# Retention and two MLPs on one core: the first two token blocks by halves of F, and all GpSimd arithmetic moved to VectorE

## The chip, the cores and the metric

The kernel runs on one core of a Trainium2 chip. A core has a matrix engine (TensorE, PE in the profile), VectorE (DVE), ScalarE (ACT), GpSimd (POOL), SyncE (SP, which here only issues transfers) and 16 DMA engines. The metric is the device time of one execution in microseconds (us). The kernel before takes 1208.26 us, the median of 3 runs (1207.79 to 1208.29).

## The reference

Three steps follow one another, all in fp32 on the outside. Step one is a retention (linear attention with decay) over B = 4 sequences of S = 768 tokens, H = 8 heads of D = 64:

```python
gamma = 1.0 - 2.0 ** (-5.0 - np.arange(H))
state = gamma * state + outer(k[t], v[t])      # per batch and head, D x D
y[t] = (1 / sqrt(D)) * q[t] @ state
```

Its output, 3072 tokens by 512, goes through two MLPs with 2048 hidden units, each with weights of its own:

```python
h = x @ w_in;  g = h - tanh(h);                 x = g @ w_out
h = x @ w_in;  g = where(h > 0, h, exp(min(h, 0)) - 1);  out = g @ w_out
```

[...]

## The kernel before, in words

Tokens are cut into NB = 6 blocks of 512, and the 2048 hidden units F into NF = 16 pieces of 128. An *iteration* n is one piece f of one block b of one MLP: 96 iterations for the first MLP (ph 0), then 96 for the second (ph 1). An iteration has a *first product* h = w_in·x of 12 matmuls (line 251: four pieces of the model dimension, three products each, since every fp32 operand is held as a high and a low part), an activation on ScalarE and VectorE (for ph 0 the chain of lines 271 to 284), a split of the result g into high part (ScalarE, line 260) and low part (line 264), and a *second product* of 12 matmuls that adds into four accumulator banks (line 317). The second product of iteration n stands on TensorE two iterations later (SKEW = 2), so TensorE's queue reads first(n), second(n-2), first(n+1), second(n-1) and so on. There are two banks for h.

Retention runs in 24 *steps* s of 128 tokens of one sequence; four steps make a block. A step has scores k·q (line 166, into banks a0 and a1), the decay mask that VectorE multiplies in on the way to the tile pt (line 175), the output, which is the old state times the scaled q (line 187, from the second block on) plus pt times v (line 195, into bank a0), and the new state k·v (line 214, bank a1; line 240 adds it). q is scaled by qtab (line 137), k by ktab (line 151), and the state by gtab (line 237). Steps 0 to 3 run ahead of the first iteration; steps 4 to 7 inside iterations 3, 6, 9 and 12; the rest four iterations apart. The output of a step is split into high and low part (lines 203 and 204) and becomes x of its block.

Each of the 64 weight pieces, a *job*, arrives by DMA as raw 64-bit words (fetch, line 76) and is converted in place. ScalarE rescales the high word to 32 bits (convert_a, line 81); VectorE shifts and masks it, puts the sign back, and puts in three bits of the low word (convert_b, lines 88, 92 and 96); ScalarE and GpSimd split the result into high part (line 108) and low part (line 109). Jobs of the first MLP are converted two in each iteration of block 0; those of the second MLP during the last block of the first and the first block of the second.

GpSimd also has: most scalings of q and k, the scaling of the state, the low part of g in the blocks where weights are converted (line 264 with lo_engine), and the low part of the second MLP's x (line 347). Where the first MLP's block is done, `finish` copies the four accumulators out on ScalarE and writes them to DRAM (x1d), from where `load_x1` reads them for the second MLP.

The order of the work on each engine is the order in which the program issues it: the loop at lines 505 to 563, the tables `todo` (which jobs in which iteration) and `events` (which retention work in which iteration), and generators that are started at one place (the matmuls) and run on at a later one (the work on VectorE and ScalarE). A tile whose buffer is still in use makes the instruction that writes it wait, and so all that is queued behind it on that engine.

## Time and profile before

| | before |
|---|---|
| median of 3 runs | 1208.26 us |
| the profiled execution: its own time, its span | 1206.79 us, 1205.0 us |
| TensorE (PE) busy | 1162.2 us, 96% |
| weight loads (PEld) busy | 948.9 us, 79% |
| VectorE (DVE) busy | 725.6 us, 60% |
| ScalarE (ACT) busy | 624.6 us, 52% |
| GpSimd (POOL) busy | 269.1 us, 22% |
| mean granted clock of TensorE | 0.980 |

The profile is of one execution. A row of a timeline gives the start in us from the start of the span, the duration in us, the engine, the line of the kernel, the operation, the tile written and those read, shapes, and how many like instructions were merged (x12); square brackets tell how long the engine was idle just before and what ended that. Matmuls are pipelined and their ends are modelled, so TensorE's pace is read from starts, not from durations. PEclk is the granted clock of TensorE as a share: 1.0 and 0.5 are its two levels, 2.4 and 1.2 GHz.

### The profile page before, as it was taken

The numbers are of one execution on the slowest core, as the hardware profiler recorded it, in microseconds if no ns is written. First come the engines' busy times: TensorE is split into PE (matmuls) and PEld (weight loads), VectorE is DVE, ScalarE is ACT, GpSimd is POOL, SyncE is SP. The second block draws the span as 40 slices with busy tenths as digits, with TensorE's granted clock in tenths as the row PEclk, the third lists the DMA queues.
The fourth block names the chain that finished last, engine by engine and source line by source line (L and its number), as shares of the span: only waits on it lengthen the run. The fifth ranks groups of instructions, "written<-read, shape, count | busy, mean of one in ns | idle before, by whom it ended". The sixth has DMA issues, their size and how long they took to land.

```text
span 1205.0 us, 15832 instructions
## 1 busy us (share of the span) xinstructions
PE 1162.2 (96%) x6039; PEld 948.9 (79%) x6039; DVE 725.6 (60%) x1008; ACT 624.6 (52%) x1089; POOL 269.1 (22%) x197
## 2 busy tenths in 40 slices
PE   6778899999999999999999999999999999999998
PEld 4556788888888888888887788888888888888886
DVE  5899975655656655655599999434344334344332
ACT  2655655445455444555677766544544454544444
POOL 3565641110111110000267567101000010010000
PEclk9778899999999999999999999999999999999999
DMA  9732102202011200100365500200200200200000
GB/s 364 290 140 70 36 27 79 71 27 79 36 36 61 79 27 27 62 27 1 124 229 166 179 2 1 70 1 1 70 1 1 70 1 1 70 1 1 35 1 35
DMA packets 26412, 78.36 MB, mean 65 GB/s; under 512 B 3040, under 2 KB 3040, under 8 KB 26336
## 3 DMA queue, kind: packets, MB, share of 16 engines
q1 hardware_dynamic: 25760, 76.56, 18.3%
q8 instruction: 47, 0.77, 0.3%
q10 hardware_dynamic: 576, 0.79, 0.2%
q14 instruction: 29, 0.24, 0.1%
HBM read 64.76 MB, written 12.58 MB: 64 GB/s over the span
## 4 chain that ended last, share of the span: by engine, by line
PE 86%; DVE 7%; DMA 4%; issue 2%; ACT 1%; SPq 0%; ACTq 0%; DVEq 0%
PE h L251 40%; PE acc L317 40%; DMA raw<-w 3%; PE sc L166 2%; DVE w L96 2%; PE o L187 2%; PE o L195 1%; DVE v L277 1%; DVE w L92 1%; DVE v L284 1%; DVE h L283 1%; DVE v L280 1%; DMA dtab<-dtab 1%; DVE w L88 1%; DMA stage<-qkv 1%
## 5 line engine op out<-in xcount | busy, mean ns | idle before, releaser
L251 PE MATMUL h<-x,w 128*128 128x512 f32 x1152 | 290.5, 403 | 13.3 <-DVE v L284 13.3
L317 PE MATMUL acc<-g,w 128*128 128x512 f32 x1152 | 279.5, 391 | 0.0
L251 PE MATMUL h<-y,w 128*128 128x512 f32 x1152 | 276.8, 389 | 1.3 <-DVE v L284 1.3
L317 PE MATMUL acc<-w,g 128*128 128x512 f32 x1152 | 276.7, 389 | 0.6 <-DVE g L264 0.6
L251 PEld LDWEIGHTS h<-x,w 128*128 128x128 f32 x1152 | 222.0, 195 | 63.8 <-DVE v L284 14.8
L251 PEld LDWEIGHTS h<-y,w 128*128 128x128 f32 x1152 | 216.2, 188 | 46.6 <-DVE v L284 1.7
L317 PEld LDWEIGHTS acc<-w,g 128*128 128x128 f32 x1152 | 216.1, 188 | 45.9 <-DVE g L264 1.0
L317 PEld LDWEIGHTS acc<-g,w 128*128 128x128 f32 x1152 | 214.8, 188 | 45.9 <-ACT g L260 0.7
L297 DVE SCALAR_TENSOR_TENSOR v<-v,t 128x512 f32<-128x512 f32 x96 | 77.2, 804 | 274.2 <-ACT t L295 274.1
L292 ACT ACTIVATE u<-h 128x512 f32<-128x512 f32 x96 | 57.5, 599 | 252.4 <-PE h L251 252.1
L277 DVE SCALAR_TENSOR_TENSOR v<-v,u 128x512 f32<-128x512 f32 x96 | 78.6, 819 | 173.1 <-ACT v L272 173.0
L271 ACT ACTIVATE u<-h 128x512 f32<-128x512 f32 x96 | 57.4, 598 | 238.8 <-issue 207.9
L260 ACT ACTIVATE g<-v 128x512 fp32r<-128x512 f32 x192 | 118.3, 616 | 18.0 <-DVE v L284 15.7
L264 DVE TENSOR_TENSOR g<-v,g 128x512 fp32r<-128x512 f32 x145 | 121.4, 837 | 0.8 <-ACT g L260 0.8
L264 POOL TENSOR_TENSOR g<-v,g 128x512 fp32r<-128x512 f32 x47 | 69.1, 1470 | 170.4 <-ACT g L260 79.7
L109 POOL TENSOR_TENSOR w<-w,w 128x512 fp32r<-128x512 f32 x64 | 101.5, 1597 | 14.4 <-ACT w L108 11.3
L347 POOL TENSOR_TENSOR y<-x,y 128x512 fp32r<-128x512 f32 x24 | 34.2, 1425 | 304.0 <-ACT y L346 304.0
L284 DVE COPY_PREDICATED v<-m,h 128x512 f32<-128x512 uint16 x96 | 70.7, 736 | 7.1
L272 ACT ACTIVATE v<-u,qa_b 128x512 f32<-128x512 f32 x96 | 69.5, 724 | 4.3
L275 ACT ACTIVATE m<-u,xs_b 128x512 bf16<-128x512 f32 x96 | 68.1, 709 | 0.0
L280 DVE SCALAR_TENSOR_TENSOR v<-v,h 128x512 f32<-128x512 f32 x96 | 65.3, 680 | 1.9 <-ACT t L274 1.8
L283 DVE TENSOR_TENSOR h<-h,t 128x512 f32<-128x512 f32 x96 | 66.2, 689 | 0.0
(43 smaller groups left out, 863.9 us busy)
## 6 DMA issues: line engine op xcount, KB each, us to landing
raw<-w SPq DMA_DIRECT2D x64, 512.0 KB, 5.5
qk<-qkv SPq DMA_DIRECT2D x20, 512.0 KB, 4.2
v<-qkv SPq DMA_DIRECT2D x24, 256.0 KB, 4.4
x1d<-o SPq DMA_DIRECT2D x12, 512.0 KB, 3.5
x<-x1d SPq DMA_DIRECT2D x12, 512.0 KB, 6.1
kn<-qkv SPq DMA_DIRECT2D x20, 256.0 KB, 6.4
out<-o SPq DMA_DIRECT2D x10, 512.0 KB, 4.8
stage<-qkv SPq DMA_DIRECT2D x4, 512.0 KB, 7.0
```

The lines of the kernel that those rows point to most:

```text
L109: nc.gpsimd.tensor_tensor(out=t[:, 1, :], in0=w, in1=t[:, 0, :].bitcast(F32), op=ALU.subtract)
L251: nc.tensor.matmul(out=h, lhsT=w[:, a, c * P:(c + 1) * P], rhs=x[:, b, c, :], start=(i == 0), stop=(i == 3 * KC - 1),)
L260: nc.scalar.activation(out=t[:, 0, :], in_=g, func=AF.Copy)
L264: engine.tensor_tensor(out=t[:, 1, :], in0=g, in1=t[:, 0, :].bitcast(F32), op=ALU.subtract)
L272: nc.scalar.activation(out=v, in_=u, func=AF.Square, bias=qa_b)
L275: nc.scalar.activation(out=big, in_=u, func=AF.Relu, bias=xs_b)
L277: lambda: nc.vector.scalar_tensor_tensor(out=v, in0=v, scalar=QB, in1=u, op0=ALU.add, op1=ALU.mult),
L280: lambda: nc.vector.scalar_tensor_tensor(out=v, in0=v, scalar=C2, in1=h, op0=ALU.mult, op1=ALU.mult),
L283: lambda: nc.vector.tensor_tensor(out=h, in0=h, in1=th, op=ALU.subtract),
L284: lambda: nc.vector.copy_predicated(out=v, mask=big.bitcast(U16), data=h),
L297: lambda: nc.vector.scalar_tensor_tensor(out=v, in0=v, scalar=1.0, in1=th, op0=ALU.add, op1=ALU.mult),
L317: nc.tensor.matmul(out=acc[e], lhsT=lhsT, rhs=rhs, start=(f == 0 and i == 0), stop=(f == NF - 1 and i == 2),)
```

## The change

- For the first two blocks, F is cut in two halves of FA = 8 pieces. The order of the first 32 iterations is block 0 with f = 0..7, block 1 with f = 0..7, block 0 with f = 8..15, block 1 with f = 8..15. After its first half a block's accumulators are copied out and written to x1d (`finish_part`); after its second half they are added to what lies in x1d by a DMA that accumulates, issued from GpSimd's queue (`finish_rest`, and `finish` for block 1).
- Jobs follow that order. From iteration 0 on two jobs are converted per iteration, from iteration 5 on one.
- Steps 4 to 7 now run in iterations 1, 3, 5 (step 4 starts ahead of the loop), steps 8 to 11 in iterations 22, 24, 26 and 28, the rest four apart as before.
- GpSimd has no arithmetic left: lines 107, 135, 149, 237, 264 and 347 of the new kernel run on VectorE.
- convert_a uses the function Prelu with a negative slope of -2^32 instead of Copy: a negative word comes out positive with 32 added to its exponent field, and the shift by 3 moves that bit to the place of the sign. So convert_b has two operations instead of three.
- The decay mask dtab carries the whole decay and scale for pt, so scores use the unscaled q, and q is scaled only for the product with the state, behind the mask on VectorE; steps 0 to 3 need no scaled q at all.
- In the loop, scores and output are both issued behind the first product of their iteration, and what VectorE and ScalarE do for them is issued at the start of the next iteration. k of a step is scaled behind the activation of its scores' iteration.

On TensorE around step 16 (iterations 49 and 50; sc16 are its scores, h0_49 and h0_50 the first products, o16 its output, acc32 the accumulators of block 2), the kernel before has:

```order
L166 MATMUL sc16_0_3203<-qk16_2986 128x128 [waits DMAHW0_49,PE_49,Pool_49]
...
L251 MATMUL h0_49_3213<-x3_2437,w0_1_280 128x512 [waits DVE_49]
...
L317 MATMUL acc32_0_2462<-g47_3174,w1_15_1340 128x512 [waits Activation_49]
...
L251 MATMUL h0_50_3263<-x3_2437,w0_2_310 128x512 [waits DVE_49]
...
L187 MATMUL o16_3276<-qk16_2986,st0_358 64x128 [waits DVE_49]
```

and the changed kernel has, from the same place on:

```order
L251 MATMUL h0_49_3193<-x3_2429,w0_1_249 128x512 [waits DVE_49]
...
L164 MATMUL sc16_0_3207<-qk16_3147 128x128 [waits DMAHW2_49,PE_49]
...
L317 MATMUL acc32_0_2454<-g47_3170,w1_15_1782 128x512 [waits Activation_49]
...
L251 MATMUL h0_50_3255<-x3_2429,w0_2_419 128x512 [waits DVE_49]
...
L187 MATMUL o16_3268<-qk16_3147,st0_315 64x128 [waits DVE_49,PE_49]
```

The scores moved behind the first product of iteration 49, so one first product less lies between them and the output.

On VectorE at the same place (v48 and v49 are the activations of iterations 48 and 49, pt16 the masked scores), the kernel before has:

```order
L284 COPY_PREDICATED v48_3170<-m48_3171,h0_48_3155 128x512 [waits DVE_49,Activation_49]
L175 TENSOR_TENSOR pt16_3202<-sc16_0_3203,dtab_88 128x512 [waits PE_49]
L175 TENSOR_TENSOR pt16_3202<-sc16_1_3204,dtab_88 128x512 [waits PE_49]
L277 SCALAR_TENSOR_TENSOR v49_3230<-v49_3230,u49_3228 128x512 [waits Activation_49]
L264 TENSOR_TENSOR g48_3234<-v48_3170,g48_3234 128x512 [waits Activation_49]
```

and the changed kernel has:

```order
L277 SCALAR_TENSOR_TENSOR v49_3219<-v49_3219,u49_3217 128x512 [waits Activation_49]
L264 TENSOR_TENSOR g48_3223<-v48_3166,g48_3223 128x512 [waits PE_49,Activation_49]
L280 SCALAR_TENSOR_TENSOR v49_3219<-v49_3219,h0_49_3193 128x512 [waits DVE_49,Activation_49]
L283 TENSOR_TENSOR h0_49_3193<-h0_49_3193,t49_3218 128x512
L284 COPY_PREDICATED v49_3219<-m49_3220,h0_49_3193 128x512 [waits DVE_49,Activation_49]
L149 TENSOR_TENSOR kn16_3149<-kn16_3149,ktab_89 128x512 [waits DMAHW0_49]
L173 TENSOR_TENSOR pt16_3206<-sc16_0_3207,dtab_88 128x512 [waits PE_49]
L173 TENSOR_TENSOR pt16_3206<-sc16_1_3208,dtab_88 128x512 [waits PE_49]
L135 TENSOR_TENSOR qk16_3147<-qk16_3147,qtab_87 128x512 [waits DMAHW7_49]
```

The mask moved from ahead of the activation of iteration 49 to behind it, with the scaling of k ahead of it and that of q behind it.

On VectorE in iteration 1, where two jobs are converted (w32 tiles are converted words, w0_3 and w1_1 finished weights), the kernel before has:

```order
L277 SCALAR_TENSOR_TENSOR v1_435<-v1_435,u1_433 128x512 [waits Activation_49]
L88 TENSOR_SCALAR w32_0_5_410<-w32_0_5_410 128x512 [waits Pool_49]
L280 SCALAR_TENSOR_TENSOR v1_435<-v1_435,h0_1_420 128x512 [waits DVE_49,Activation_49]
L88 TENSOR_SCALAR w32_1_3_412<-w32_1_3_412 128x512 [waits Pool_49]
L283 TENSOR_TENSOR h0_1_420<-h0_1_420,t1_434 128x512
L92 SCALAR_TENSOR_TENSOR w32_0_5_410<-raw0_5_159,w32_0_5_410 128x512 [waits DMAHW1_49,DVE_49]
L284 COPY_PREDICATED v1_435<-m1_436,h0_1_420 128x512 [waits DVE_49,Activation_49]
L92 SCALAR_TENSOR_TENSOR w32_1_3_412<-raw1_3_161,w32_1_3_412 128x512 [waits DMAHW2_49]
L96 SCALAR_TENSOR_TENSOR w32_0_5_410<-raw0_5_159,w32_0_5_410 128x512 [waits DVE_49]
L96 SCALAR_TENSOR_TENSOR w32_1_3_412<-raw1_3_161,w32_1_3_412 128x512 [waits DVE_49]
```

and the changed kernel has:

```order
L277 SCALAR_TENSOR_TENSOR v1_473<-v1_473,u1_471 128x512 [waits Activation_49]
L264 TENSOR_TENSOR g0_477<-v0_413,g0_477 128x512 [waits Activation_49]
L280 SCALAR_TENSOR_TENSOR v1_473<-v1_473,h0_1_447 128x512 [waits DVE_49,Activation_49]
L93 TENSOR_SCALAR w32_0_4_433<-w32_0_4_433 128x512
L283 TENSOR_TENSOR h0_1_447<-h0_1_447,t1_472 128x512
L93 TENSOR_SCALAR w32_1_2_435<-w32_1_2_435 128x512
L284 COPY_PREDICATED v1_473<-m1_474,h0_1_447 128x512 [waits DVE_49,Activation_49]
L94 SCALAR_TENSOR_TENSOR w32_0_4_433<-raw0_4_155,w32_0_4_433 128x512 [waits DMAHW7_49]
L94 SCALAR_TENSOR_TENSOR w32_1_2_435<-raw1_2_157,w32_1_2_435 128x512 [waits DMAHW0_49,DVE_49]
L107 TENSOR_TENSOR w0_3_481<-w32_0_3_359,w0_3_481 128x512 [waits Activation_49]
L107 TENSOR_TENSOR w1_1_483<-w32_1_1_361,w1_1_483 128x512 [waits Activation_49]
```

Two operations of the conversion went, and the low parts of g and of two weights came from GpSimd.

The diff, cut to its core:

```diff
+FA = 8
+NEG = -(2.0 ** 32)
-        nc.scalar.activation(out=w, in_=raw[job].bitcast(F32)[:, 1::2], func=AF.Copy, scale=REBIAS)
+        nc.scalar.activation(out=w, in_=raw[job].bitcast(F32)[:, 1::2], func=AF.Prelu, scale=REBIAS, alpha=NEG)
...
-            lambda: nc.vector.tensor_scalar(
-                out=wu, in0=wu, scalar1=3, scalar2=0x7FFFFFF8,
-                op0=ALU.logical_shift_left, op1=ALU.bitwise_and,
-            ),
-            lambda: nc.vector.scalar_tensor_tensor(
-                out=wu, in0=r[:, 1::2], scalar=0x80000000, in1=wu,
-                op0=ALU.bitwise_and, op1=ALU.bitwise_or,
-            ),
+            lambda: nc.vector.tensor_single_scalar(wu, wu, 3, op=ALU.logical_shift_left),
...
-        nc.gpsimd.tensor_tensor(
+        return lambda: nc.vector.tensor_tensor(
             out=t[:, 1, :], in0=w, in1=t[:, 0, :].bitcast(F32), op=ALU.subtract
...
             nc.vector.tensor_tensor(out=pt[:, j], in0=sc[j], in1=dtab[:, j], op=ALU.mult)
+        if s >= B:
+            att_scale_q(s)
...
+                if m == 1 and b == 1:
+                    nc.gpsimd.dma_start(out=dst[:, sl, :], in_=o[:, sl, :], accum_op=ALU.add)
+                else:
+                    nc.sync.dma_start(out=dst[:, sl, :], in_=o[:, sl, :])
+    def finish_part(b):
+        o = att.tile([P, 2, TB], F32, tag="qk", name=f"part{b}")
+        for e in range(2):
+            nc.scalar.activation(out=o[:, e, :], in_=acc[e], func=AF.Copy)
+        nc.sync.dma_start(out=x1d[b][:, 0:2, :], in_=o)
+        for e in range(2, 4):
+            o = att.tile([P, TB], F32, tag="v", bufs=B, name=f"part{b}_{e}")
+            nc.scalar.activation(out=o, in_=acc[e], func=AF.Copy)
+            nc.sync.dma_start(out=x1d[b][:, e, :], in_=o)
+    def finish_rest(b):
+        for e in range(4):
+            o = att.tile([P, TB], F32, tag="v", bufs=B, name=f"rest{b}_{e}")
+            nc.scalar.activation(out=o, in_=acc[e], func=AF.Copy)
+            nc.gpsimd.dma_start(out=x1d[b][:, e, :], in_=o, accum_op=ALU.add)
...
-            at = [3 + 3 * k, 4 + 3 * k, 4 + 3 * k] if b == 0 else [4 * k + 1, 4 * k + 2, 4 * k + 2]
+            if b == 0:
+                at = 2 * k - 1
+            elif b == 1:
+                at = FA + NF - 2 + 2 * k
+            else:
+                at = b * NF + 4 * k + 1
...
+        order = [(0, b, f, lo, hi) for lo, hi in ((0, FA), (FA, NF)) for b in range(2) for f in range(lo, hi)]
+        order += [(0, b, f, 0, NF) for b in range(2, NB) for f in range(NF)]
+        order += [(1, b, f, 0, NF) for b in range(NB) for f in range(NF)]
...
+        for ph, b, f, flo, fhi in order:
+            for g in gens:
+                run(g)
...
+            h = first_mm(2 * ph, xhl[ph * NB + b], f, n)
+            for g, *args in events.get(n, []):
+                gens.append(g(*args))
+                next(gens[-1], None)
+            v, chain = (act_elu if ph else act_tanhshrink)(h, n, flush)
+            halves = [convert_c(job) for job in prev_jobs]
+            side = []
+            interleave_into(side, [convert_b(j) for j in jobs])
+            side += halves
+            if prev_v is not None:
+                side.insert(0, lambda: split_lo(g_t[n - 1], prev_v))
+            interleave(chain, side)
+            if n in scale_k:
+                att_scale_k(scale_k[n])
...
-    dtab = causal * (g_pj.T[None] ** -(t[:, None, None] + 1.0))[..., None]
+    lag = np.maximum(t[None, :] - t[:, None], 0.0)[:, None, None, :]
+    dtab = causal * scale * g_pj.T[None, :, :, None] ** lag
```

## Rows read from the trace of the kernel before

**Rows 1.** The page, part 1: busy time, share of the span, instructions.
```profile
PE 1162.2 (96%) x6039; PEld 948.9 (79%) x6039; DVE 725.6 (60%) x1008; ACT 624.6 (52%) x1089; POOL 269.1 (22%) x197
```

**Rows 2.** Busy time by stretch: us of each engine, PEclk, DMA share, GB/s.
```profile
31.30:157.10 125.80, 101.07 (x570) 81.13 (x569) 122.44 (x155) 76.27 (x129) 77.43 (x53) 0.85 0.35 131
157.10:633.60 476.50, 476.50 (x2785) 389.46 (x2784) 298.62 (x455) 250.64 (x435) 74.08 (x61) 1.00 0.19 62
62.80:69.60 6.80, 5.99 (x18) 4.38 (x20) 6.80 (x9) 4.32 (x8) 5.21 (x4) 0.50 0.00 0
670.00:677.00 7.00, 5.75 (x26) 4.44 (x25) 6.73 (x11) 4.04 (x7) 2.77 (x3) 1.00 0.39 145
```

**Rows 3.** Who waited for whom: us in total, times, longest.
```profile
PE h L251 <- DVE v L284: 14.6, 5, 6.8
ACT w L81 <- POOL w L109: 17.1, 21, 1.8
```

**Rows 4.** Timeline of TensorE around a step, blocks 1 and 2.
```profile
273.98 2.88 PE L317 MATMUL acc<-g,w 128*128 128x512 f32 x12
276.79 1.16 PE L166 MATMUL sc<-qk 64*128 64x128 f32 x16
277.88 3.02 PE L251 MATMUL h<-x,w 128*128 128x512 f32 x12
280.74 2.88 PE L317 MATMUL acc<-g,w 128*128 128x512 f32 x12
283.46 2.88 PE L251 MATMUL h<-x,w 128*128 128x512 f32 x12
...
288.78 0.96 PE L317 MATMUL acc<-g,w 128*128 128x512 f32 x3
```

**Rows 5.** Timeline of VectorE in the same stretch.
```profile
275.62 0.69 DVE L277 SCALAR_TENSOR_TENSOR v<-v,u 128x512 f32<-128x512 f32 x1 [2.10 <-ACT v L272]
276.23 0.68 DVE L264 TENSOR_TENSOR g<-v,g 128x512 fp32r<-128x512 f32 x1
...
278.22 0.74 DVE L284 COPY_PREDICATED v<-m,h 128x512 f32<-128x512 uint16 x1
278.86 1.27 DVE L175 TENSOR_TENSOR pt<-sc,dtab 128x512 f32<-128x512 f32 x2
```

**Rows 6.** All instructions of line 88: duration in ns, shortest, median, longest.
```profile
L88 DVE TENSOR_SCALAR w<-w x64: 411/920/1522, 14.4 to 755.5; 128x512 uint32<-128x512 uint32 x64
```

**Rows 7.** Timeline of VectorE ahead of the first iteration.
```profile
14.84 0.69 DVE L92 SCALAR_TENSOR_TENSOR w<-raw,w 128x512 uint32<-128x512 uint32 x1
...
19.00 0.69 DVE L204 TENSOR_TENSOR x<-o,x 128x512 fp32r<-128x512 f32 x1 [1.80 <-ACT x L203]
```

**Rows 8.** Timeline of ScalarE: a conversion at the start, an evacuation of accumulators.
```profile
17.84 0.65 ACT L81 ACTIVATE w<-raw 128x512 f32<-128x512 f32 x1
...
283.86 2.05 ACT L330 ACTIVATE o<-acc 128x512 f32<-128x512 f32 x4
```

**Rows 9.** Timeline of GpSimd at the start: waits for transfers.
```profile
17.94 1.27 POOL L137 TENSOR_TENSOR stage<-stage,qtab 128x512 f32<-128x512 f32 x1 [1.28 <-DMA stage<-qkv]
...
25.79 4.40 POOL L151 TENSOR_TENSOR kn<-kn,ktab 128x512 f32<-128x512 f32 x4 [0.45 <-DMA kn<-qkv]
```

**Rows 10.** Timeline of TensorE: first iterations, and the end of the first MLP.
```profile
31.30 7.69 PE L251 MATMUL h<-x,w 128*128 128x512 f32 x24
...
63.61 0.80 PE L251 MATMUL h<-x,w 128*128 128x512 f32 x1 [3.27 <-DVE v L284]
...
642.09 4.61 PE L251 MATMUL h<-x,w 128*128 128x512 f32 x12 [2.86 <-DVE v L284]
...
672.46 3.01 PE L251 MATMUL h<-y,w 128*128 128x512 f32 x12 [1.25 <-DVE v L284]
```

**Rows 11.** DMA issues by line: count, size, median us from issue to landing.
```profile
x1d<-o SPq DMA_DIRECT2D x12, 512.0 KB, 3.5
v<-qkv SPq DMA_DIRECT2D x24, 256.0 KB, 4.4
```

More of the change, by code (lines that the diff above doesn't have):

```diff
@@ L372, in retention_moe_kernel @@
         jobs0 = [(0, 0), (0, 1)]
[L373 to L375 removed]
+        for lo, hi in ((0, FA), (FA, NF)):
+            for f in range(lo, hi):
+                jobs0 += [(0, f + 2)] * (f + 2 < hi) + [(1, f)]
+            if hi < NF:
+                jobs0 += [(0, hi), (0, hi + 1)]
         nc.scalar.dma_start(out=dtab, in_=ins["dtab"])
@@ L439, in retention_moe_kernel @@
         out_pe(2)
-        conv(1)
         run(g_sc[3])
+        lo1()
+        run(g_out[2])
         convert_a(jobs0[3])
-        run(g_out[2])
         out_pe(3)
+        for s in range(B):
+            att_scale_k(s)
         run(g_out[3])
-        for s in range(B):
-            att_scale_k(s, nc.gpsimd)
-        conv(2, 3)
-        convert_a(jobs0[4])
-        convert_a(jobs0[5])
-        conv(4, 5)
-        att_scale_q(B, nc.gpsimd)
-        todo = {}
-        rest = jobs0[6:]
-        for f in range(NF):
-            todo[f] = rest[:2]
-            rest = rest[2:]
-        assert not rest
+        pairs = [att_state_pair(j) for j in range(2)]
+        for g in pairs:
+            next(g)
+        for g in pairs:
+            run(g)
+        att_load_v(B)
+        att_load_kn(B)
+        scores_pe(B)
+        ops(convert_b(jobs0[2]))
+        run(g_sc[B])
+        att_scale_k(B)
+        ops(convert_b(jobs0[3]))
+        todo = {}
+        rest = jobs0[4:]
+        n = 0
+        while rest:
+            k = 2 if n < FA - 3 else 1
+            todo[n] = rest[:k]
+            rest = rest[k:]
+            n += 1
         base = (NB - 1) * NF
@@ new lines, in second @@
+                elif pf == hi - 1:
+                    finish_part(pb)
+        order = [(0, b, f, lo, hi) for lo, hi in ((0, FA), (FA, NF)) for b in range(2) for f in range(lo, hi)]
+        order += [(0, b, f, 0, NF) for b in range(2, NB) for f in range(NF)]
+        order += [(1, b, f, 0, NF) for b in range(NB) for f in range(NF)]
+        n = 0
+        for ph, b, f, flo, fhi in order:
+            first, last = b == 0, b == NB - 1
+            for g in gens:
+                run(g)
+            if n < NF:
+                for job in jobs0[12 + 2 * n:14 + 2 * n]:
+                    fetch(*job)
+            jobs = todo.get(n, [])
+            h = first_mm(2 * ph, xhl[ph * NB + b], f, n)
+            gens = []
+            for g, *args in events.get(n, []):
[11 more added lines that the diff above has]
+                att_scale_k(scale_k[n])
+            for job in todo.get(n + 1, []):
+                convert_a(job)
+            prev_v = v
+            prev_jobs = jobs
+            pend.append((2 * ph + 1, f, n, b, flo, fhi))
+            if ph == 0 and last:
+                fetch(2, f)
+            second(SKEW)
+            if n in load:
+                load_step(load[n])
+            if n in load_v:
+                att_load_v(load_v[n])
+            nxt = 0 if ph == 0 and last else b + 1 if ph else None
+            if nxt is not None and nxt < NB:
+                if f == 6:
+                    load_x1(nxt)
+                if 8 <= f < 8 + KC:
+                    split_x1(nxt, f - 8)
+            n += 1
```

146 lines of the change are left out of this document (46 added, 100 removed).

## The prediction, made before the changed kernel was run

> **What bounds the kernel now.** I read the page first, then stretches, then TensorE's waits, then timelines. By the page TensorE is busy 96% of the span, VectorE 60%, GpSimd 22% [rows 1]. A share over the whole span hides the stages, so I cut it. From 157.1 to 633.6 us TensorE has no idle time at clock 1.00 and VectorE is busy 299 of 476 us; from 31.3 to 157.1 us, the first 14 iterations, VectorE is busy 122 of 126 us and TensorE's clock is 0.85 [rows 2]. The longest waits of TensorE are for line 284, the end of the activation on VectorE [rows 3]. So the start is VectorE's, the rest TensorE's.
>
> *TensorE's own price.* A product of 12 matmuls takes 2.72 us from start to start (280.74 to 283.46), so an iteration takes 5.44. A step costs four pieces more [rows 4]. The product at 273.98 would be over at 276.70, and the next one starts at 277.88: 1.18 for the scores, and 0.14 because the product behind them takes 2.86. The product at 283.46 would be over at 286.18, the next starts at 288.78: 2.60 for output and state, and again 0.14. That is 4.06 a step.
>
> *What is lost now.* At 157.10 TensorE starts the first product of iteration 14. It has done 14 first and 12 second products and four steps: 26 x 2.72 + 4 x 4.06 = 87.0 us in 125.8, so 38.8 us are lost in the start. At the end of the first MLP it waits 2.86 and 1.25 us for line 284 [rows 10], and the slower clock behind the first wait makes it about 6.
>
> **The change part by part.**
>
> *Conversions and GpSimd's work.* Line 88 takes 411 ns alone and up to 1522 [rows 6]; the merge of line 92 takes 0.69 alone [rows 7]. The long ones lie beside GpSimd's instructions. The Trainium skill, page "SBUF — State Buffer", section "Who interferes with whom", says that VectorE instructions in a two-port mode or with two SBUF inputs and GpSimd exclude each other for a whole instruction. Rows 6 fit that; by the rule every shift would take its 0.41 in the changed kernel, by the median of rows 6 0.92, which is 1.0 us more in each of five iterations with two jobs, so 5 us in the sum. With no GpSimd arithmetic I price independent VectorE instructions by start-to-start, 0.61 (275.62 to 276.23 [rows 5]), and a shift at 0.33 (0.41 less the same 0.08 of overlap). An iteration with two jobs has the activation's four instructions, the low part of g, two shifts, two merges and two low parts of weights: 9 x 0.61 + 2 x 0.33 = 6.1 us. Those of odd iterations 1, 3 and 5 also scale k, mask twice and scale q, 4 x 0.61: 8.6. Even ones have the output's low part and two instructions on the state, about 1.5, and wait some 1.35 us for ScalarE, whose two conversions (0.65 each [rows 8]) need the buffers that the low parts of weights free (the same wait before: line 81 for GpSimd, 17.1 us in 21 times [rows 3]). TensorE needs 2 x 5.44 + 4.06 = 14.9 for such a pair.
>
> *Start.* By the issue order the raw word of weight (0,1) has 4.75 MB ahead or in it, stage 3 of the kernel before 5.0 MB and its first k 8.0 MB; those landed by 17.94 and 25.79 [rows 9], so I put this one at 17.3. ScalarE converts it ahead of the first evacuation, so VectorE's first line 204 starts at 18.6 (19.00 before [rows 7]). Then 17 instructions of 0.61 and a shift, with the scaling of k that GpSimd did in 4.40 us [rows 9]: 29.2. Scores of step 4 follow, and the first product starts at 30.4, against 31.30 [rows 10]. Moving four tables and the scaling of q away therefore gains 0.9 us here and no more.
>
> *Iterations 0 to 7.* The two first products before took 7.69 us from 31.30, more than 5.44: part at half clock. I end the first one at 35.0. The activation's first VectorE instruction comes 1.64 us after a product's end (275.62 less 273.98 [rows 4, 5]): 36.6. Iteration 0 ends on VectorE with the state of step 4 at 45.0, and only then are a0 and a1 free for the scores of step 5. Iteration 1 needs 8.6: output of step 5 at 53.6. Output and state, a second and a first product: 2.60 + 2.86 + 2.72 = 8.2, to 61.8; scores of step 6 wait for the state until 62.0. Then 1.6 + 8.6: output of step 6 at 71.9, and 8.2 more: 80.1. Iteration 5 has one job less (0.94): output of step 7 at 89.4; 8.2 and one second product: the first product of iteration 8 starts at 100.3. TensorE idles four times for 2 to 5 us in this. After an idle 3.27 us at 63.61 the clock stood at 0.50 for the 6.8 us of rows 2; after 1.25 us at 672.46 it stayed at 1.00 [rows 2, 10]. Half clock for 6.8 us is 3.4 us of products. Most such stretches lie inside waits for VectorE; I charge one: 103.7.
>
> *What that gains.* From there to the state of 157.1 us six first and six second products are missing (steps 4 to 7 are done): 32.6 us. It is reached at 136.3, a gain of 20.8.
>
> *Iterations 8 to 21.* One job: 4 + 1 + 1 + 1 instructions of 0.61 and a shift, 4.6 us, under 5.44: hidden. Without that cover each excess would be paid by TensorE. The two evacuations more, 2.05 us on ScalarE [rows 8], lie beside a first product of 2.72: nothing. More wait is only that the banks come free some 0.4 us ahead of need.
>
> *Steps 8 to 19.* This part costs. Behind the scores TensorE now has one second and one first product: 1.18 + 2.86 + 2.72 = 6.76, and 0.09 to the output: 6.85 us after the end of the first product. VectorE reaches line 284 at 4.24 (278.22 less 273.98), the next instruction 0.64 later (278.86 [rows 5]); behind it now stand the scaling of k, both masks and the scaling of q: 4.24 + 0.64 + 3 x 0.61 + 0.69 = 7.40, and 0.07 to TensorE: 7.47. TensorE waits 0.62. Step 8 has one job in its iteration: two half operations of conversion and a low part more, 1.9. So 11 x 0.62 + 1.9 = 8.7 us lost that were not before. Steps 20 to 23 scale no k: nothing.
>
> *Second MLP's weights.* With two jobs in two iterations and the split of x, VectorE comes to 6 us against 5.44 once or twice; a first product may follow up to 2.5 us later without waiting. I leave 1 of the 6 us: a gain of 5.
>
> *The accumulating writes.* No row shows one. Bounds: 0, as the plain write of 3.5 us [rows 11] is hidden, to what the last rival prices. I take 0: nothing reads x1d for 50 iterations, and the buffers have about 6 us more than a v load of 4.4 [rows 11] needs.
>
> *The rectifier.* No row shows one. Bounds: the 0.65 of line 81 [rows 8], and twice that if it took two passes: 42 us more on ScalarE, which is idle for 580 us of the span [rows 1], but up to 1.3 of it in each early iteration would be waited for, some 6 us. I take 0.65, the nearest row.
>
> *SP's queue.* Loads of a step are issued two iterations ahead of its scores, 10.9 us of TensorE's time against a landing of 4.4 [rows 11]; k of steps 0 to 3 stands ahead of six weights that it stood behind. Nothing, beyond what the start has; if a load were late its step would wait for the rest.
>
> **Sum.** The profiled execution took 1206.79 us, of which 1205.0 are span; the median of the runs is 1.5 above it. -20.8 - 5 + 8.7 = -17.1: 1189.7 for an execution like the profiled one, 1191.2 for the median. I say 1191.
>
> **The rivals.**
>
> *TensorE bounds from iteration 0 on.* For it: VectorE's sum per pair, 6.1 + 2.4 + 6.1 + 1.5 = 16.1, is near 14.9, and the steps' 0.62 is a difference of two sums of five terms. Against: the wait for a0 and a1. From 30.4, 14 products, four steps and 2.7 for half clock give iteration 8 at 87.4 in place of 103.7, and without the 8.7: 1191 - 16.3 - 8.7 = 1166. Half of that, 1178, is as good a reading of it.
>
> *The clock falls at each of five early waits.* For it: a mean clock of 0.85 over 125.8 us [rows 2] means 0.15 / 0.5 x 125.8 = 38 us at half, five to six stretches of 6.8. Four more at 3.4: 1191 + 13.6 = 1205. Against: a slow TensorE lets VectorE catch up.
>
> *The accumulating writes hold buffers (slower).* Six such writes leave GpSimd's queue one behind the other. The load of v for step 10 needs the first one's buffer, and x of block 3 needs that of block 1's result. Counted from the end of iteration 25's first product, v of step 10 is wanted at 16 (pieces of rows 4), the copies end at 5 and the load takes 4.4; x of block 3 is wanted 9.7 after its copies. With L us for each write, step 10 waits L - 6.6, and x of block 3 waits 2L - 9.7. The total 3L - 16.3 passes the gain of 17 and 2.4 more at L = 12: from there on the kernel is slower. At 15 us it is 1191 + 28.7 = 1220. Against: 3.5 us for a plain write of 512 KB. The same page of the Trainium skill, section "SBUF: two separate sides", warns that a DMA issued from GpSimd can be held up while VectorE holds the shared port, 620 ns becoming 3100. No row here shows it, since GpSimd issued none. By that ratio 3.5 us would be 17.5, an estimate, and the sum about 1227.
>
> *The rectifier isn't in the loaded function set.* One load of 1.3 us stands in the trace, and the changed kernel's order has one as well, so two loads a job are unlikely; 128 of them would put ScalarE over 5.44 us and the time above 1250. It gets 0.02.
>
> **How the numbers follow.** Forecast 0.56, its own range 1182 to 1200; TensorE-bound 0.23; clock 0.13; accumulating writes 0.06; function loads 0.02. A difference of 0.2%, 2.4 us, is about what can be told from none here. Faster: the first two and most of the third, 0.90; same: the rest of the third, 0.03; slower: 0.07. The range leaves out the lower half of the second case and the last two: 1173 to 1204.
>
> **What would show it.** Right: no GpSimd row but DMAs; line 93 near 0.41 everywhere; iteration 8's first product near 104 us; waits of TensorE for line 135 of about 0.6 us, eleven of them; the end of the first MLP almost without waits. Wrong: an early iteration at TensorE's pace; waits for line 135 gone or over 1 us; ScalarE or SP waiting for an accumulating DMA; the clock at half for long after 50 us.

## The result, and the profile of the changed kernel

The changed kernel takes 1189.13 us (median of 4 runs, 1187.96 to 1189.76) against 1208.28 us of the kernel before on the same chip (4 runs, 1207.79 to 1208.57): a ratio of 0.9841, with a 95% interval of 0.9824 to 0.9858. The forecast was 1191. The profiled execution of the changed kernel took 1187.96 us, of which 1186.2 are span; that is 18.8 less than the profiled execution before. The terms below are set against these two. An execution several times as long as the others of its kernel is left out of the ratios; there is one, of 6571.74 us, at the last experiment.

The page, part 1, of the changed kernel (it answers to [rows 1]):

```profile
PE 1152.7 (97%) x6038; PEld 943.5 (80%) x6039; DVE 682.8 (58%) x1133; ACT 624.0 (53%) x1097; POOL 5.6 (0%) x10
```

VectorE has 125 instructions more and 43 us less busy time. The work of GpSimd came on top of its own, one instruction for each weight went, and the sum is done sooner.

All instructions of the new shift (line 93) and of the rectifier (line 86), with the shortest, median and longest duration in ns (to set beside [rows 6, 8]):

```profile
L93 DVE TENSOR_SCALAR w<-w x64: 410/420/427, 12.0 to 737.1; 128x512 uint32<-128x512 uint32 x64
L86 ACT ACTIVATE w<-raw x64: 647/659/687, 11.3 to 730.3; 128x512 f32<-128x512 f32 x64
```

The shift took 411 to 1522 ns before, with a median of 920; now the longest of the 64 takes 427. By the medians that is 64 x 0.50 = 32 us of VectorE's busy time. The Trainium skill, page "SBUF — State Buffer", section "Who interferes with whom", has VectorE and GpSimd shut each other out of their shared port for whole instructions. The trace agrees, 420 against 920 ns at the median. The rectifier costs what a copy does, 0.66 us.

Where the 18.8 us came from can be read from the starts of first products that stand at the same place in both programs. The timeline of TensorE in the changed kernel, from left: start in us, duration, line, tile, count:

```profile
135.65 0.61 PE L251 MATMUL h<-x,w 128*128 128x512 f32 x2
...
253.65 0.62 PE L251 MATMUL h<-x,w 128*128 128x512 f32 x2
...
653.85 2.43 PE L251 MATMUL h<-y,w 128*128 128x512 f32 x10
```

and the one of these in the kernel before that was not shown yet:

```profile
271.26 1.07 PE L251 MATMUL h<-x,w 128*128 128x512 f32 x4
```

| first product of iteration | before | changed | gained since the row above |
|---|---|---|---|
| 0 | 31.30 | 31.24 | 0.06 |
| 14 | 157.10 | 135.65 | 21.39 |
| 32 | 271.26 | 253.65 | -3.84 |
| 96 | 672.46 | 653.85 | 1.00 |
| end of the span | 1205.0 | 1186.2 | 0.19 |

So all of the gain, and a little more, arises in the first 14 iterations; a part is paid back in the steps that follow, and the end of the first MLP returns some of that.

TensorE's longest waits in the changed kernel: in all, times, longest (to set beside [rows 3]):

```profile
PE o L187 <- DVE qk L135: 16.2, 15, 2.9
PE sc L164 <- DVE x L204: 4.8, 1, 4.8
```

The waits for the activation's end, 14.6 us before, are not there. In their place the outputs of the steps wait for the scaled q (line 135), 15 times.

### The profile page after: what moved, and what is told of

It reads as the page before. It is cut to its first block, busy times and chain, and to the rows that moved or that the text cites. A ratio compares the mean times of both kernels' runs of the same rounds, so it can differ in the third digit from the quotient of the medians.

```text
span 1186.2 us, 15678 instructions
## 1 busy us (share of the span) xinstructions
PE 1152.7 (97%) x6038; PEld 943.5 (80%) x6039; DVE 682.8 (58%) x1133; ACT 624.0 (53%) x1097; POOL 5.6 (0%) x10
## 3 DMA queue, kind: packets, MB, share of 16 engines
q1 hardware_dynamic: 26048, 76.56, 18.6%
## 4 chain that ended last, share of the span: by engine, by line
PE 83%; DVE 8%; issue 4%; ACT 2%; DMA 2%; ACTq 0%; DVEq 0%; SPq 0%
PE acc L317 41%; PE h L251 38%; PE o L187 2%; PE o L195 2%; DVE pt L173 2%; DVE v L284 1%; DVE kn L149 1%; ACT v L272 1%; DVE v L280 1%; DVE qk L135 1%; DVE h L283 1%; DMA kn<-qkv 1%; ACT u L271 1%; DMA raw<-w 1%; DMA gtab<-gtab 1%
## 5 line engine op out<-in xcount | busy, mean ns | idle before, releaser
L251 PE MATMUL h<-x,w 128*128 128x512 f32 x1152 | 277.7, 390 | 0.0
L251 PEld LDWEIGHTS h<-x,w 128*128 128x128 f32 x1152 | 216.5, 188 | 45.3 <-ACT w L106 0.2
L297 DVE SCALAR_TENSOR_TENSOR v<-v,t 128x512 f32<-128x512 f32 x96 | 66.5, 693 | 299.6 <-ACT t L295 299.6
L277 DVE SCALAR_TENSOR_TENSOR v<-v,u 128x512 f32<-128x512 f32 x96 | 66.4, 692 | 161.4 <-ACT v L272 161.3
L264 DVE TENSOR_TENSOR g<-v,g 128x512 fp32r<-128x512 f32 x192 | 131.5, 685 | 0.8 <-ACT g L260 0.8
L300 DVE TENSOR_TENSOR v<-h,v 128x512 f32<-128x512 f32 x96 | 65.7, 684 | 0.0
L293 ACT ACTIVATE v<-u 128x512 f32<-128x512 f32 x96 | 60.6, 631 | 3.1
L295 ACT ACTIVATE t<-u 128x512 f32<-128x512 f32 x96 | 59.2, 617 | 0.0
```

The source lines that it names most:

```text
L251: nc.tensor.matmul(out=h, lhsT=w[:, a, c * P:(c + 1) * P], rhs=x[:, b, c, :], start=(i == 0), stop=(i == 3 * KC - 1),)
L264: nc.vector.tensor_tensor(out=t[:, 1, :], in0=g, in1=t[:, 0, :].bitcast(F32), op=ALU.subtract)
L277: lambda: nc.vector.scalar_tensor_tensor(out=v, in0=v, scalar=QB, in1=u, op0=ALU.add, op1=ALU.mult),
L297: lambda: nc.vector.scalar_tensor_tensor(out=v, in0=v, scalar=1.0, in1=th, op0=ALU.add, op1=ALU.mult),
```

## The experiments

All times of this part stand against runs of the kernel before on the same chip, 1206.70 to 1206.82 us. On one of these chips the changed kernel was timed once more:

> The changed kernel once more, unchanged, on the chip of this call, to have it beside the kernels of the experiments: its ratio to the kernel before is expected within 0.2% of 0.984.

It took 1188.35 us, ratio 0.9853 (0.984 to 0.9866). The two measurements, 0.9841 and 0.9853, are the scatter to keep in mind below.

### The scaling of k behind mask and q

The prediction charged 8.7 us for instructions ahead of q in VectorE's queue. One of them, the scaling of k, is needed only later. This moves it behind:

```diff
                 run(g)
+            if n - 1 in scale_k:
+                att_scale_k(scale_k[n - 1])
             if n < NF:
...
             interleave(chain, side)
-            if n in scale_k:
-                att_scale_k(scale_k[n])
```

> The changed kernel with one move: the scaling of k of a step stands behind the mask and the scaling of q on VectorE, not ahead of them. Theory (TensorE's wait for the scaled q is a queue on VectorE, and every instruction in it costs its 0.6 us in full): the eleven waits of 0.56 us for steps 9 to 19 vanish, step 8's falls from 1.90 to 1.3, those of steps 5 to 7 by 0.6 each: 0.56 x 11 + 0.6 + 1.8 = 8.6 us off 1189.1, 1180.5. Rival (the wait turns into another one, of the state product for the scaled k, or of the next iteration): 1189 within 2.4.

It took 1177.54 us, ratio 0.9759 (0.9746 to 0.9772): 10 to 11 less than the changed kernel. The waits of the output:

```profile
PE o L187 <- DVE qk L135: 5.8, 4, 1.7
```

Eleven of fifteen are gone. The place can be seen at one step. TensorE in the changed kernel, at step 12 (in brackets the idle time before, and who ended it):

```profile
269.30 1.09 PE L187 MATMUL o<-qk,st 64*64 64x128 f32 x16 [0.57 <-DVE qk L135]
```

VectorE of the changed kernel, beside it:

```profile
266.05 0.74 DVE L284 COPY_PREDICATED v<-m,h 128x512 f32<-128x512 uint16 x1
266.69 0.67 DVE L149 TENSOR_TENSOR kn<-kn,ktab 128x512 f32<-128x512 f32 x1
267.28 1.28 DVE L173 TENSOR_TENSOR pt<-sc,dtab 128x512 f32<-128x512 f32 x2
268.48 0.68 DVE L135 TENSOR_TENSOR qk<-qk,qtab 128x512 f32<-128x512 f32 x1
```

The same place in the experiment, TensorE:

```profile
263.92 1.09 PE L187 MATMUL o<-qk,st 64*64 64x128 f32 x16
```

and VectorE:

```profile
261.91 1.27 DVE L173 TENSOR_TENSOR pt<-sc,dtab 128x512 f32<-128x512 f32 x2
263.10 0.68 DVE L135 TENSOR_TENSOR qk<-qk,qtab 128x512 f32<-128x512 f32 x1
263.69 0.68 DVE L149 TENSOR_TENSOR kn<-kn,ktab 128x512 f32<-128x512 f32 x1
```

k took one place of 0.6 us ahead of q, and TensorE stood for 0.57; with k behind q the output has no idle time ahead of it. The theory held: it was the order on VectorE, and the wait did not turn into another. Iteration 8 starts at 99.79 in place of 103.01, 3.2 earlier, where 1.8 was expected of steps 5 to 7. The rest is the clock: at step 6 TensorE stands at half clock in the changed kernel (from 73.40 to 76.80, shown further down, which costs 1.6 us there), and in this execution at 1.00 in the same stretch. So 1 to 2 of the 10 to 11 us are not the order's.

### The scores ahead of the first product

The other way to give VectorE time: from step 12 on TensorE does the scores one product earlier, so that the masks can run before the activation.

```diff
+            soon = [g(*args) for g, *args in here if g is att_scores and args[0] >= 3 * B]
+            for g in soon:
+                next(g, None)
             h = first_mm(2 * ph, xhl[ph * NB + b], f, n)
...
+            for g in soon:
+                run(g)
             v, chain = (act_elu if ph else act_tanhshrink)(h, n, flush)
```

> The changed kernel, but from step 12 on the scores stand ahead of the first product of their iteration on TensorE, and mask and scaling of q ahead of that iteration's activation on VectorE, as in the kernel before. Theory (the place of the scores makes the wait): the eight waits of 0.56 us of steps 12 to 19 vanish, those of steps 5 to 11 stay: 4.5 us off, 1184.6. Rival (the wait is the price of VectorE doing GpSimd's scalings, wherever they stand): 1189 within 2.4, with the waits still there.

It took 1185.53 us, ratio 0.9824 (0.981 to 0.9837), 2 to 3 less than the changed kernel. At the steps it did what was expected: TensorE waits for line 135 seven times (10.1 us) in place of 15, and from iteration 32 to 96 the trace shows 395.5 us where the changed kernel needs 400.2. That is 4.7 for the 4.5 expected. The total shows less, because iteration 8 started at 104.76 in this execution, 1.7 later than in the changed kernel, and two more stretches of TensorE ran at half clock:

```profile
93.80:97.20 3.40, 3.40 (x33) 3.06 (x28) 3.40 (x7) 0.86 (x2) 0.00 (x0) 0.50 0.02 5
192.80:196.20 3.40, 3.40 (x37) 3.07 (x35) 3.32 (x6) 1.39 (x4) 0.00 (x0) 0.50 0.26 64
```

(columns as in [rows 2]). Half clock for 3.4 us of work is 1.7 us lost, so the first of them is as long as the whole delay at iteration 8. Both lie ahead of step 12, in a part of the program that the edit doesn't touch.

### Three VectorE instructions for each weight

The sign could also be carried as before: a plain copy on ScalarE, and a mask and a merge more on VectorE.

```diff
-        nc.scalar.activation(out=w, in_=raw[job].bitcast(F32)[:, 1::2], func=AF.Prelu, scale=REBIAS, alpha=NEG)
+        nc.scalar.activation(out=w, in_=raw[job].bitcast(F32)[:, 1::2], func=AF.Copy, scale=REBIAS)
...
+            lambda: nc.vector.scalar_tensor_tensor(
+                out=wu, in0=r[:, 1::2], scalar=0x80000000, in1=wu,
+                op0=ALU.bitwise_and, op1=ALU.bitwise_or,
+            ),
```

> The changed kernel with the old conversion: ScalarE's Copy in place of the rectifier, and three VectorE operations per job instead of two. Theory (in iterations 0 to 6 VectorE's queue is what TensorE waits for, and in 8 to 21 one job leaves it 0.7 us under 5.44): 0.61 more for each of 15 early jobs, 9 us, some 3 us where 8 to 21 go over 5.44, and 1 to 4 at the end of the first MLP: 1189 + 10 to 16, about 1201. Rival (VectorE is idle 42% of the span, so a tenth of its work more is hidden): 1189 within 2.4.

It took 1199.21 us, ratio 0.9933 (0.9919 to 0.9946): 11 more than the changed kernel. Its waits (its lines stand seven lower, line 142 is the scaling of q and 211 the low part of x):

```profile
PE o L194 <- DVE qk L142: 20.2, 15, 4.4
PE sc L171 <- DVE x L211: 6.7, 1, 6.7
```

Iteration 8 starts at 111.30, 8.3 later. These waits grew by 5.9 us; the clock stood at half in two more stretches of 3.4 us (from 58.70 and from 99.50), which can make up to 1.7 each of the 8.3. So where VectorE sets the pace, an instruction more for each weight is paid: without the rectifier 11 of the 19 us are gone, given the rest of the change.

### The low parts of the weights back on GpSimd

```diff
-        return lambda: nc.vector.tensor_tensor(
+        return lambda: nc.gpsimd.tensor_tensor(
             out=t[:, 1, :], in0=w, in1=t[:, 0, :].bitcast(F32), op=ALU.subtract
```

> The changed kernel, but the low parts of the 64 weights are subtracted on GpSimd, as before. Theory (GpSimd's instructions block VectorE's that read two SBUF operands or run two elements a cycle): VectorE gives away 0.61 per job but its shifts go from 0.42 towards 0.9 and merges from 0.68 towards 0.9, and the buffers of converted words come free a GpSimd instruction of 1.3 to 1.6 us later: slower by 4 to 12 us, about 1197. Rival (VectorE's sum of work is all that counts): 64 x 0.61 less work, some of it in the early iterations: 1184.

It took 1188.55 us, ratio 0.9849 (0.9836 to 0.9863): no difference, and both expectations failed. Busy time in three stretches (of PE, PEld, DVE, ACT, POOL, with counts; then PEclk, DMA share, GB/s), the changed kernel:

```profile
20.00:105.00 85.00, 68.36 (x530) 55.10 (x530) 69.78 (x125) 43.56 (x76) 0.00 (x0) 0.92 0.59 231
105.00:180.00 75.00, 75.00 (x332) 62.12 (x332) 63.85 (x111) 59.16 (x105) 0.00 (x0) 1.00 0.16 57
570.00:760.00 190.00, 190.00 (x840) 157.39 (x839) 140.88 (x241) 134.53 (x240) 0.00 (x0) 1.00 0.38 122
```

and the experiment:

```profile
20.00:105.00 85.00, 69.50 (x528) 56.10 (x528) 67.22 (x110) 44.44 (x76) 20.49 (x15) 0.90 0.58 229
105.00:180.00 75.00, 75.00 (x333) 62.10 (x332) 64.26 (x97) 58.86 (x105) 17.51 (x14) 1.00 0.17 57
570.00:760.00 190.00, 190.00 (x840) 157.34 (x839) 145.10 (x209) 135.07 (x240) 45.72 (x32) 1.00 0.38 122
```

VectorE has 61 instructions fewer (416 for 477) and is busy for 276.6 us in place of 274.5. What it no longer does, it loses on the others. All its shifts in the experiment, and its merges of the first 180 us:

```profile
L93 DVE TENSOR_SCALAR w<-w x64: 409/420/1295, 12.0 to 737.5; 128x512 uint32<-128x512 uint32 x64
L94 DVE SCALAR_TENSOR_TENSOR w<-raw,w x30: 666/1213/1281, 12.4 to 175.7; 128x512 uint32<-128x512 uint32 x30
```

Most shifts still take 0.42, but the longest takes 1.30 where it takes 0.43 in the changed kernel: long shifts as in [rows 6] are back. The merge has a median of 1213 ns, in the changed kernel one of 682 over the same 180 us and 693 at the longest. So the two effects cancel, the work taken off VectorE and the lengthening of what stays; iteration 8 starts at 103.34 against 103.01.

### Without the halves of F

```diff
-FA = 8
+FA = 16
```

(with the five places that assume two halves.)

> The changed kernel without the halves: blocks 0 and 1 run through all 16 pieces of F one after the other, so two jobs are converted in each of iterations 0 to 12; no partial results, no accumulating writes; everything else as changed. Theory (two jobs in an iteration are more than VectorE and ScalarE get done in TensorE's 5.44 us): iterations 8 to 12 take some 7.5 us instead of 5.44, 10 us, and one or two more stretches at half clock: 1189 + 10 to 15, about 1201. Rival (the cheaper conversion and the earlier steps made the gain, not the halves): 1189 within 2.4.

It took 1203.60 us, ratio 0.9971 (0.9961 to 0.9982). Without the order by halves 14 to 16 of the 18 to 19 us are gone. The timeline shows why; TensorE in iterations that still convert two weights each:

```profile
118.29 2.56 PE L251 MATMUL h<-x,w 128*128 128x512 f32 x10 [0.97 <-DVE w L107]
...
126.44 2.56 PE L251 MATMUL h<-x,w 128*128 128x512 f32 x10 [0.98 <-DVE w L107]
```

These two products, of neighbouring iterations, are 8.15 apart, where TensorE's own work is 5.44. Beside them, ScalarE and VectorE:

```profile
118.27 1.26 ACT L86 ACTIVATE w<-raw 128x512 f32<-128x512 f32 x2 [2.99 <-DVE w L107]
...
120.80 0.69 DVE L277 SCALAR_TENSOR_TENSOR v<-v,u 128x512 f32<-128x512 f32 x1 [1.97 <-ACT v L272]
```

ScalarE's two conversions wait for the low parts of weights on VectorE (line 107), which free their buffers; ScalarE's part of the activation (line 272) is queued behind the conversions, VectorE waits for that, and its next low parts are queued behind it. This ring lasts 8.15. In all ScalarE waits 13 times for line 107, 41.4 us, in the changed kernel 5 times, 17.1. Iteration 8 starts at 105.64, only 2.6 later than with halves, and up to 1.7 of that can be a stretch at half clock (from 94.30 to 97.70) that the changed kernel doesn't have. So halves hardly make the first iterations quicker; they spare the next ones, because iterations 8 to 21 then convert one weight each and run at TensorE's pace.

### Plain writes in place of accumulating ones

The second half's result overwrites the first's, issued from SyncE; the addition of the first half of F in blocks 0 and 1 is left out.

```diff
-            nc.gpsimd.dma_start(out=x1d[b][:, e, :], in_=o, accum_op=ALU.add)
+            nc.sync.dma_start(out=x1d[b][:, e, :], in_=o)
```

(and the same at the other place.)

> The changed kernel with plain writes from SyncE's queue in place of the six accumulating ones from GpSimd's; left out is the addition of the first half of F in blocks 0 and 1. Theory (ScalarE's one wait of 3.9 us for an accumulating write is hidden): 1189 within 1, the wait shorter. Rival (held buffers cost TensorE time): faster by 2 to 4.

It took 1188.88 us, ratio 0.9851 (0.9837 to 0.9866): no change. The accumulating writes of the changed kernel, by issue, count, size and median us to landing, beside its plain ones (to set beside [rows 11]):

```profile
x1d<-o SPq DMA_DIRECT2D x8, 512.0 KB, 3.4
...
x1d<-rest POOLq DMA_DIRECT2D x4, 256.0 KB, 7.2
x1d<-o POOLq DMA_DIRECT2D x2, 512.0 KB, 7.3
```

They take about twice as long, and one wait for them stands in the changed kernel's trace, on ScalarE:

```profile
ACT x L203 <- DMA x1d<-o: 3.9, 1, 3.9
```

The experiment's trace has no such wait and its time is the same: from iteration 8 to iteration 96 it needs 550.90 us, the changed kernel 550.84. So those 3.9 us were hidden.

### The first evacuation ahead of the second weight

Ahead of the first iteration VectorE stands idle for 5.5 us, behind a conversion on ScalarE that waits for its weight. The edit puts that conversion behind the evacuations of steps 0 and 1:

```diff
         lo0 = convert_c(jobs0[0])
-        convert_a(jobs0[1])
         run(g_out[0])
...
-        ops(convert_b(jobs0[1]))
         run(g_out[1])
+        convert_a(jobs0[1])
+        ops(convert_b(jobs0[1]))
```

> The changed kernel with one move ahead of the loop: ScalarE converts the raw word of weight (0,1) behind the evacuations of steps 0 and 1, not ahead of them, so VectorE's first line 204 need not wait 5.5 us for that word to land. Theory (the start is VectorE's queue from there on, but k of step 4 lands at 36 us and holds iteration 0 next): the first product starts 3 to 4 us earlier, of which 1 to 2 are left at iteration 8: 1187.5. Rival A (the queue alone decides): 4 us off, 1185. Rival B (transfers decide): nothing off.

It took 1190.69 us, ratio 0.9864 (0.9848 to 0.9879): nothing gained. VectorE in the changed kernel:

```profile
18.65 0.69 DVE L204 TENSOR_TENSOR x<-o,x 128x512 fp32r<-128x512 f32 x1 [5.50 <-ACT x L203]
...
36.08 0.69 DVE L149 TENSOR_TENSOR kn<-kn,ktab 128x512 f32<-128x512 f32 x1 [3.05 <-DMA kn<-qkv]
```

and in the experiment:

```profile
14.42 0.69 DVE L204 TENSOR_TENSOR x<-o,x 128x512 fp32r<-128x512 f32 x1 [1.25 <-ACT x L203]
...
35.31 0.69 DVE L149 TENSOR_TENSOR kn<-kn,ktab 128x512 f32<-128x512 f32 x1 [3.18 <-DMA kn<-qkv]
```

The first evacuation is 4.2 us earlier and the chain meets later waits; where it scales k of step 4 it is 0.77 ahead, and it stood there for the transfer either way. The output of step 5 is still 0.78 ahead (53.94 against 54.72), and a stretch at half clock from 53.50 to 56.90, which the changed kernel doesn't have, takes that back: iteration 8 starts at 103.75 against 103.01. So of 4.2 us some 0.8 were left at the transfer of k, and the order in which SyncE's queue issues the transfers is the next thing to move.

### The three together: order of transfers, evacuation, k behind q

So k and v of step 4 were put ahead of four weights in SyncE's queue, with a fifth buffer for the 32-bit words, and the edits of the first and the last experiment added:

```diff
-    stg = ctx.enter_context(tc.tile_pool(name="stg", bufs=4))
+    stg = ctx.enter_context(tc.tile_pool(name="stg", bufs=5))
...
-        for job in jobs0[4:12]:
+        for job in jobs0[4:8]:
             fetch(*job)
...
         att_load_kn(B)
+        for job in jobs0[8:12]:
+            fetch(*job)
```

> Meant to be faster than both kernels: k of a step scaled behind its q (as in the first run), the evacuations ahead of the conversion of weight (0,1), v and k of step 4 loaded ahead of four weights instead of behind them, and five buffers for converted words instead of four. Theory: 9.9 off for the first by its run, 3 to 6 for the early part, since VectorE no longer waits 3 us for k of step 4, nor ScalarE as long for a buffer: 1187.6 - 9.9 - 4.5 = 1173 on the chip where the kernel before takes 1206.8. Rival (transfers into the first 40 us hold whatever is moved): no more than the first run, 1178.

It took 1174.21 us, ratio 0.9736 (0.9721 to 0.9751), 14 us under the changed kernel. k of step 4 is scaled 4.2 us earlier than in the changed kernel and without a wait:

```profile
31.84 0.68 DVE L149 TENSOR_TENSOR kn<-kn,ktab 128x512 f32<-128x512 f32 x1
```

and iteration 8 starts 7.1 us earlier:

```profile
95.92 1.30 PE L251 MATMUL h<-x,w 128*128 128x512 f32 x5
```

3.2 of these 7.1 the first experiment had by itself. Over that one the ratio is 0.9736 against 0.9759, which is 2.8 us, with intervals that overlap at their edges; what the order of transfers, the evacuations and the fifth buffer each bring to it was not separated.

### Mask, q and k ahead of the conversions

On top of the last version, in iterations that hold the scores of a step and convert weights, VectorE does mask, q and k right behind the activation and the conversions after them:

```diff
+            if jobs and any(g is att_scores for g, *_ in events.get(n, [])):
+                interleave(chain, first_side)
+                for g in gens:
+                    run(g)
+                gens = []
+                att_scale_k(scale_k.pop(n))
+                ops(side)
```

> The combined kernel with one more move, in iterations 1, 3, 5 and 22, where scores and conversions meet: mask, scaling of q and then of k stand right behind the activation on VectorE, ahead of the shifts, merges and low parts of that iteration's jobs. Theory (two reasons for the early waits: the order in VectorE's queue, and its sum of 16 us per pair of iterations against TensorE's 15): the waits for the scaled q, 7.7 us in 4 times, nearly vanish, but part comes back one iteration later, since the sum stays: 3 us off, 1171. Rival A (the order alone): 7 off, 1167. Rival B (the sum alone): 1174 within 2.

It took 1174.40 us, ratio 0.9729 (0.9717 to 0.9742): no difference. The last version's waits of TensorE:

```profile
PE o L187 <- DVE qk L135: 7.7, 4, 2.3
...
PE sc L164 <- DVE x L204: 2.9, 1, 2.9
```

and this one's:

```profile
PE sc L164 <- DVE x L204: 5.9, 3, 2.9
```

The waits for q are all gone, but the conversions that now come later hold up the low part of x and the state of the step, and the scores of the next step wait for that. Iteration 8 starts at 98.06. This fits the rival by which the sum of VectorE's work, and no longer its order, decides in the early iterations once k stands behind q, but it does not show it: the clock was at half for longer in this execution than in the last one (20.4 us in three stretches up to 67 us, where the last one has two of 3.4), and the first product alone starts 1.2 us later (31.33 against 30.14), so more than half of the 2.1 us at iteration 8 can be the clock's.

## Why the prediction was right, step by step

**GpSimd and the conversions.** The shift at 0.41 everywhere held (410 to 427 ns), and so did the price of an independent VectorE instruction, 0.61 from start to start: the rows of step 12 read 266.05, 266.69, 267.28, which is 0.64 and 0.59.

**The start.** Forecast 30.4 for the first product, measured 31.24: of the gain of 0.9 us that stood here, 0.06 came. The first evacuation on VectorE was put at 18.6 and came at 18.65. Behind it VectorE waited once for TensorE, whose state products ran at a granted clock of 0.51 from 25.70 to 29.10:

```profile
29.41 0.69 DVE L228 COPY st<-dsp 128x512 f32<-128x512 f32 x1 [0.61 <-PE dsp L214]
```

Then the forecast's walk from instruction to instruction has two errors that nearly cancelled. It let the first product run until 35.0, partly at half clock; the product ran at full clock, and TensorE was at the next instruction at 34.19. And it had no wait for a load ("Nothing, beyond what the start has"), but VectorE stood 3.05 us for k of step 4, until 36.08, so that it began the activation of iteration 0 at 37.76, where the walk has 36.6:

```profile
37.76 0.68 DVE L277 SCALAR_TENSOR_TENSOR v<-v,u 128x512 f32<-128x512 f32 x1
```

In the version whose k is there in time (the three together) this instruction starts at 34.58, 3.2 us earlier, and the first product only 1.1 earlier. The state of step 4, forecast for 45.0, was done at 46.08. That the error is no larger than 1.1 is luck.

**Iterations 0 to 7.** TensorE in the changed kernel, at the four waits of the forecast's walk and at iteration 8:

```profile
45.28 2.93 PE L164 MATMUL sc<-qk 64*128 64x128 f32 x16 [4.77 <-DVE x L204]
...
54.72 1.09 PE L187 MATMUL o<-qk,st 64*64 64x128 f32 x16 [2.91 <-DVE qk L135]
...
73.13 1.75 PE L187 MATMUL o<-qk,st 64*64 64x128 f32 x16 [2.81 <-DVE qk L135]
...
77.25 3.02 PE L317 MATMUL acc<-g,w 128*128 128x512 f32 x12
...
92.20 1.09 PE L187 MATMUL o<-qk,st 64*64 64x128 f32 x16 [2.45 <-DVE qk L135]
...
94.71 3.02 PE L317 MATMUL acc<-g,w 128*128 128x512 f32 x12
...
103.01 1.29 PE L251 MATMUL h<-x,w 128*128 128x512 f32 x5
```

The forecast had 45.0, 53.6, 71.9, 89.4 and 103.7: four waits of 2 to 5 us, by the engine and the lines that it named. The outputs came 1.1, 1.2 and 2.8 late. The first 1.1 is the late activation: from 46.00, where it begins that of iteration 1, VectorE works without a gap (8.50 of 8.50 us to 54.50) until it has the scaled q of step 5. The other 1.6 is the clock. At half, by stretch:

```profile
42.70:49.50 6.80, 4.15 (x19) 3.43 (x20) 5.48 (x12) 5.61 (x10) 0.00 (x0) 0.50 0.97 393
...
73.40:76.80 3.40, 3.40 (x38) 3.07 (x35) 3.40 (x8) 1.77 (x4) 0.00 (x0) 0.50 0.92 372
```

The first cost nothing: TensorE was through with the work that it slowed, and then idle for 2.91 us, before q of step 5 was there. The second lies on output and state of step 6, which take 4.12 us to the second product behind them (73.13 to 77.25), where those of step 7 take 2.51 (92.20 to 94.71). That is 1.6 lost, and VectorE then waited 3.16 us, until 84.41, for an activation whose first product stands behind that work. So the 100.3 of the walk, 1.1 and 1.6 give the 103.0. The forecast charged 3.4 for one long stretch; the long one was hidden, a short one cost 1.6, and the wait for k made up most of the rest. The engine, the lines and the number of waits held; that the time of iteration 8 did within 0.7 is partly luck.

**What that gains.** The state of iteration 14 was forecast for 136.3 and came at 135.65; the gain is 21.4 where 20.8 stood.

**Iterations 8 to 21.** TensorE is busy without a gap at clock 1.00, as forecast (75.00 of 75 us in the second of the changed kernel's stretches at the GpSimd experiment).

**Steps 8 to 19.** Step 8 was to wait 1.9, and its output, at 190.71, waited 1.90. The others were to wait 0.62 and waited 0.56 (ten of them; one 0.46): 8.0 us in all, forecast 8.7. The first experiment shows the cause, since one instruction of 0.6 us, moved, takes these waits away.

**The second MLP's weights.** From 570 to 760 us TensorE is busy for 190.00 of 190 us (the third of these stretches). The table has 1.00 us of gain from iteration 32 to 96, in which 8 steps cost 8 x 0.56 = 4.5: so this term is 5.5 by difference, forecast 5.

The sum of the forecast is -17.1; by the table and these waits it is -21.4 - 5.5 + 8.0 = -18.9, against 18.8 of the two spans. Two of the three terms are taken from the table itself, so this is a check of the third alone: steps 8 to 11 wait 3.5 us, and the table loses 3.84 between iterations 14 and 32. What the difference is stays open.

**The rivals.** That TensorE bounds from iteration 0 on fell by the four waits above. The clock at five waits fell as well: two stretches behind the start, one of them hidden.

Of the accumulating writes, the sign that the prediction named did appear: ScalarE waited 3.9 us for one, at x of block 3, where the rival's 2L - 9.7 gives 4.9 at the measured 7.3. By its sum, 3L - 16.3, that would be 5.6 us of TensorE's time, and TensorE lost none: the experiment without these writes is no faster. At 275.70 ScalarE went on, and its next activation still waited 1.35 us for the first product. What the rival had wrong is that a held buffer reaches TensorE in full. The Trainium skill, page "SBUF — State Buffer", section "SBUF: two separate sides", gives a factor of five for a transfer issued from GpSimd that is held up. Here the whole difference from a plain write, the addition included, is a factor of 2.1 for 512 KB (7.3 against 3.4) and of 2.7 for 256 KB (7.2 against 2.7 for the same four in the experiment).

The rectifier needed no other function set: one load of 1283 ns stands in the trace, as before.

## What to carry to other kernels

Where an engine is short of time only in one stage, spread the work that can wait over the next stage: here 14 to 16 us of the gain went when that was taken out, and 11 when the saved instruction was. When work moves into another engine's queue, list what is queued behind it that somebody waits for, at every step; one scaling of 0.6 us ahead of the instruction that TensorE needed cost some 8 us, and putting it behind that one was free. And before taking out a wait at the start, look which transfer the chain meets next.

## What was not expected of the hardware

An accumulating write to DRAM took 7.2 us for 256 KB and 7.3 for 512 KB, a plain one 3.4 for 512 KB; so here the size hardly mattered. Sixty-four subtractions given to GpSimd saved VectorE no busy time at all (276.6 us against 274.5 in the three stretches), because other instructions of VectorE grew longer beside them.

The clock behind early waits differs between programs that differ little: after waits of 2 to 5 us it stood at 0.50 for stretches of 3.4, 6.8 or 10.2 us, or not at all, while the waits of 0.56 us every 26 left it at 1.00. What decides between these is open. A stretch of 3.4 us on TensorE's path moves iteration 8 by 1.6 to 1.7 us, as between the changed kernel and the first two experiments, and that is enough to hide or to feign an effect of 2 us of an edit.
